# Sliding-window attention and a sentence-level MoE: an FFN schedule with its short slots moved back, and another order of the load queue

## The chip, the cores and the metric

One core of a Trainium2 chip runs the whole program: a matmul engine (TensorE, PE), three engines for elementwise work and reductions (VectorE or DVE, ScalarE or ACT, GpSimd or POOL), SyncE, and 16 DMA engines that all transfers share. The metric is the device time of one launch in microseconds, here the median of three runs.

## The reference, cut to what matters

Eight sentences (batches) of 576 tokens. First comes attention with 8 heads of width 64. Heads 0 to 3 look back over a window of 32 tokens ("plain"), heads 4 to 7 over 128 tokens at every fourth one ("dual", for dilated). The result, 576 x 512 per batch, is averaged over its tokens; a gate picks one of eight experts for the whole batch; and this expert's two-layer FFN with ReLU runs on all tokens of the batch.

```python
def _attn_ref(q, k, v):                     # each (8, 8, 576, 64) f32
    scores = scale * np.matmul(q, k.transpose(0, 1, 3, 2))
    rel = pos[:, None] - pos[None, :]
    mask_plain = (rel >= 0) & (rel < 32)
    mask_dil = (rel >= 0) & (rel < 128) & (rel % 4 == 0)
    ...                                     # softmax over the masked scores
    return np.matmul(attn, v)

def _moe_ref(x, w_gate, w1, w2):            # x (8, 576, 512), w1 (8, 512, 1024), w2 (8, 1024, 512)
    pooled = x.mean(axis=1)
    logits = pooled @ w_gate
    e_idx = np.argmax(logits, axis=1)       # one expert for a whole batch
    ...
    h = np.maximum(x[mask] @ w1[e], 0.0)
    out[mask] = gate_w[mask, None, None] * (h @ w2[e])
```

So no weight of batch b can be loaded before the attention of batch b is over, its mean is taken and the gate has named an expert.

## The kernel before: slots, pieces, gate and queue

Each batch's attention is cut into four slots of two heads (slot t has batch t // 4; the first two of a batch are dual, the last two plain), and its FFN into 21 pieces: 16 of the first layer (8 column blocks x 2 halves of the tokens, four matmuls each), four of the second (128 tokens each, eight matmuls) and a tail of 64 tokens. `PIECES` says how many pieces run beside each attention slot. PE works in this order strictly.

```python
PIECES = [0] * 7 + [6, 6, 5, 2, 2] + [8, 8, 2, 3] * 7
```

FFN 0 so runs in slots 7 to 11, and FFN b in slots 4b+8 to 4b+11. Attention ends in slot 31 (the last output of it in slot 32), and slots 32 to 39 have FFN 6 and FFN 7 alone.

One slot of the main loop, cut; `pre` is the slot before, whose second half ends here:

```python
for t in range(7, len(PIECES)):
    cur, pre = sl[t], sl[t - 1]
    ...                                    # items = the pieces of this slot
    gb, gn = divmod(t - 5, NSLOT)
    if gn == 0 and 0 < gb < B:
        emit_gate(gb)                      # gate of batch b at the start of slot 4b+5
    ...
        run_T(t)                           # transposes of keys or queries for a slot to come (L267)
        pre.av_a()                         # probabilities x values, first part (L353)
        flush()                            # stores of finished output tiles
        cur.s()                            # scores (L288)
        cur.x()                            # exp (ACT)
        pre.av_b()
        if lead: items.pop(0)()
        pre.ln(); cur.mask(); pre.rd()
    for f in items[:k0]: f()
    pre.norm()                             # normalise, and sum for the mean (DVE)
    for b, g, nm in tsched.get(t + 1, []):
        if g == 0:
            emit_pair(b, nm)               # rearrange plain keys or queries on DVE (L251)
    for f in items[k0:]: f()
```

`tsched` places the transposes: dual keys of batch b in slot 4b-2, dual queries in 4b-1, plain keys in 4b, plain queries in 4b+1. For the plain ones `emit_pair` reads the loaded tile one slot earlier, on DVE.

The gate, with the loads that hang on it. All loads of the program are issued by GpSimd, one after the other, and turn f32 into bf16 on the way:

```python
def emit_gate(b):
    ...                                    # 4 matmuls, maximum and index (DVE), the index to a GpSimd register
    nc.gpsimd.dma_start(out=w1b[:, 2:4, :], ...)            # w1 of the chosen expert, L511
    for a in range(2):
        nc.gpsimd.dma_start(out=w1b[half(a), 0:2, :], ...)  # its other half in two parts, L516
    if b == 0:
        load_va(2)                         # dual values of batch 2
        load_qb(2)                         # plain keys and queries of batch 2
        load_w2(e_val, w2b)
        load_qa(3)                         # dual keys and queries of batch 3
        load_vb(2)                         # plain values of batch 2
    else:
        load_vb(b + 2)                     # plain values
        load_w2(e_val, w2b)
        load_qa(b + 3)                     # dual keys, dual queries
    load_va(b + 3)                         # dual values
    load_qb(b + 3)                         # plain keys, plain queries
```

GpSimd waits in this queue for the expert's index before it goes on to w1 of batch b and to everything listed after it.

The first layer, where w1's four row blocks are taken in the order in which they land:

```python
def ffn1(b, fc, hf, eng, cs=(2, 3, 0, 1)):
    ...
    if 2 in cs:
        s["hm"] = bank()[:, 0:HALF]        # one of three PSUM banks
    hm = s["hm"]
    for c in cs:
        ...
        nc.tensor.matmul(hm, lhsT=w[:, fc % 4, :], rhs=s["xt"][:, c, cols], start=(c == 2), stop=(c == 1))   # L573
    if 1 not in cs:
        return
    ...                                    # ReLU to bf16, on ACT or DVE
```

Of the kernel before, what the change touches and what calls it, by code (L numbers as in the profile page):

```python
# [20 lines left out]
B = 8  # L21
# [21 lines left out]
HALF = 288  # L43
NSLOT = 4
EARLY = 7

PIECES = [0] * 7 + [6, 6, 5, 2, 2] + [8, 8, 2, 3] * 7


@with_exitstack  # L50
def kernel(
# [42 lines left out]
    def bank():  # L94
        return psM.tile([P, 512], F32, name="m", tag="M", space=PSUM)[:]
# [12 lines left out]
    def load_tiles(b):  # L108
        t = {}
        for g in range(2):  # L110
            for nm in ("k", "q"):
                shape = [P, RJ, DH] if g else [P, 2, RH, DH]
                t[nm, g] = ldp.tile(shape, BF16, name=f"{nm}m{g}", tag=f"{nm}m{g}")
            t["v", g] = ldp.tile([P, 4, 4, DH], BF16, name=f"vm{g}", tag=f"vm{g}")
        t["vt", 0] = ldp.tile([KB, 4, DH], BF16, name="vt0", tag="vt0")
        t["vt", 1] = ldp.tile([KB, 4, 2, DH], BF16, name="vt1", tag="vt1")
        loads[b] = t

    def load_1(b, g, nm):
        i = src[nm][b, 4 * g : 4 * g + 4]  # L120
        if g == 0:
            i = bass.AP(tensor=i.tensor, offset=i.offset, ap=[[RH * DH, P], [2 * S * DH, 2], [1, RH * DH]])
            nc.gpsimd.dma_start(out=loads[b][nm, g][:].rearrange("p h j d -> p h (j d)"), in_=i)
        else:
            i = i.rearrange("h s d -> (h s) d").rearrange("(p j) d -> p j d", j=RJ)
            nc.gpsimd.dma_start(out=loads[b][nm, g][:], in_=i)

    def load_qk(b, g):
        for nm in ("k", "q"):
            load_1(b, g, nm)  # L130

    def load_v(b, g):
        t = loads[b]["v", g]
        if g == 0:
            for h in range(4):
                nc.gpsimd.dma_start(out=t[:, h], in_=v[b, h, 0:512, :].rearrange("(c p) d -> p c d", p=P))  # L136
        else:
            nc.gpsimd.dma_start(out=t[:], in_=v[b, 4:8, 0:512, :].rearrange("h (p j) d -> p h j d", j=4))

    def load_vt(b, g):  # L140

        vt = loads[b]["vt", g]
        if g == 0:
            nc.gpsimd.dma_start(out=vt[:], in_=v[b, 0:4, 512:S, :].rearrange("h p d -> p h d"))
        else:
            nc.gpsimd.dma_start(out=vt[:], in_=v[b, 4:8, 448:S, :].rearrange("h (p t) d -> p h t d", t=2))

    GO = (1, 0)

    def load_qa(b):  # L150
        if b < B:
            load_tiles(b)
            load_qk(b, GO[0])

    def load_va(b):
        if b < B:
            load_v(b, GO[0])
            load_vt(b, GO[0])

    def load_qb(b):  # L160
        if b < B:
            load_qk(b, GO[1])

    def load_vb(b):
        if b < B:
            load_v(b, GO[1])
            load_vt(b, GO[1])
# [75 lines left out]
    def half(a):  # L243
        return slice(64 * a, 64 * a + 64)
# [250 lines left out]
    def emit_gate(b):  # L495
        s = st[b]
        pooled = s["pooled"]
        lg = bank()[0:1, 0:E]
        for c in range(4):
            nc.tensor.matmul(lg, lhsT=pooled[:, c : c + 1], rhs=wg_t[:, c, :], start=(c == 0), stop=(c == 3))  # L500
        l_sb = small.tile([1, E], F32, name="l_sb", tag="l_sb")
        mx = small.tile([1, 8], F32, name="mx", tag="mx")
        mi = small.tile([1, 8], U32, name="mi", tag="mi")
        nc.vector.max_with_indices(mx[:], mi[:], lg)
        nc.vector.tensor_copy(out=l_sb[:], in_=lg)
        s["gate"] = (l_sb, mx)
        e_val = nc.values_load(mi[0:1, 0:1].bitcast(I32), engines=[ET.Pool], min_val=0, max_val=E - 1)
        w2b = wp.tile([P, 8, DM], BF16, name="w2b", tag="w2b")
        w1b = wp.tile([P, 4, F], BF16, name="w1b", tag="w1b")
        s["w1"], s["w2"] = w1b, w2b  # L510
        nc.gpsimd.dma_start(  # L511
            out=w1b[:, 2:4, :],
            in_=moe_w1[ds(e_val, 1), 256:512, :].rearrange("e (c p) f -> p (e c) f", p=P),
        )
        for a in range(2):
            nc.gpsimd.dma_start(  # L516
                out=w1b[half(a), 0:2, :],
                in_=moe_w1[ds(e_val, 1), 128 * a : 128 * a + 128, :].rearrange("e (h d) f -> d (e h) f", d=DH),
            )
        if b == 0:  # L520
            load_va(2)
            load_qb(2)
            load_w2(e_val, w2b)
            load_qa(3)
            load_vb(2)
        else:
            load_vb(b + 2)
            load_w2(e_val, w2b)
            load_qa(b + 3)
        load_va(b + 3)  # L530
        load_qb(b + 3)

    def load_w2(e_val, w2b):

        nc.gpsimd.dma_start(
            out=w2b[:].rearrange("p (x j) f -> p x (j f)", x=2),
            in_=moe_w2[ds(e_val, 1)].rearrange("e (x p j) f -> p (e x) (j f)", x=2, p=P),
        )
# [16 lines left out]
    def emit_gate_bc(b):  # L555

        gw = st[b]["gw"]
        gbc = small.tile([P, 1], F32, name="gbc", tag="gbc")
        nc.sync.dma_start(out=gbc[:], in_=gw[0:1, 0:1].to_broadcast([1, P]))
        st[b]["gbc"] = gbc  # L560


    def ffn1(b, fc, hf, eng, cs=(2, 3, 0, 1)):
        s = st[b]
        if fc == 0 and hf == 0 and "ht" not in s:
            s["ht"] = htp.tile([P, 8, S], BF16, name="ht", tag="ht")
        cols = slice(HALF * hf, HALF * hf + HALF)
        if 2 in cs:
            s["hm"] = bank()[:, 0:HALF]
        hm = s["hm"]  # L570
        for c in cs:
            w = s["w1"][:, c, F // 2 * (fc // 4) : F // 2 * (fc // 4) + F // 2].rearrange("p (m j) -> p j m", j=4)
            nc.tensor.matmul(hm, lhsT=w[:, fc % 4, :], rhs=s["xt"][:, c, cols], start=(c == 2), stop=(c == 1))  # L573
        if 1 not in cs:
            return
        o = s["ht"][:, fc, cols]
        if eng == "A":
            nc.scalar.activation(out=o, in_=hm, func=AF.Relu)  # L578
        else:
            nc.vector.tensor_scalar_max(out=o, in0=hm, scalar1=0.0)  # L580
# [3 lines left out]
    def flush():  # L584
        for f in stores:
            f()
        stores.clear()
# [40 lines left out]
    for b in range(B):  # L628
        for n in (0, 2):
            t = NSLOT * b + n  # L630
# [3 lines left out]
    def run_T(t):  # L634
        for b, g, nm in tsched.get(t, []):
            for f in emit_T(b, g, nm):
                f()
# [41 lines left out]

    sl = [slot(t) for t in range(len(PIECES))]  # L680

# [10 lines left out]
    nd_banks = {"0dk": (0, 1), "0pk": (0, 1), "1dk": (2, 1), "1dq": (0, 2)}  # L692
    evac = {}

    def piece(b, x, e):
        if x < 16:
            ffn1(b, x // 2, x % 2, e)
        elif x < 20:
            ffn2(b, x - 16, "AD"[x % 2])
        else:  # L700
            ffn_tail(b)
# [35 lines left out]
    done = 0  # L737
    for t in range(7, len(PIECES)):
        cur, pre = sl[t], sl[t - 1]
        n = PIECES[t]  # L740

        lead = t > 7 and n >= 5 and done % 21 < 16 and pre.on
        items = []
        for i, x in enumerate(range(done, done + n)):
            e = "A" if ((lead or t == 7) and i == 0) or 2 * i >= n else "D"
            items.append(lambda x=x, e=e: piece(x // 21, x % 21, e))
        done += n
        gb, gn = divmod(t - 5, NSLOT)
        if gn == 0 and 0 < gb < B:
            emit_gate(gb)  # L750
        if t == 7:
            items.pop(0)
            n -= 1
            dve, act = emit_T(2, GO[0], "q")
            dve()
            act()
        else:
            run_T(t)
            pre.av_a()
            flush()  # L760
            if (t == 8) if gb == 0 else gn == 2 and gb < B:
                emit_gate_bc(gb)
            cur.s()
            cur.x()
            if pre.on and not cur.on:
                items.pop(0)()
                n -= 1
            pre.av_b()
            if lead:
                items.pop(0)()  # L770
                n -= 1
            pre.ln()
            cur.mask()
            pre.rd()
        k0 = n // 2
        for f in items[:k0]:
            f()
        if t > 7:
            pre.norm()
        for b, g, nm in tsched.get(t + 1, []):  # L780
            if g == 0:
                emit_pair(b, nm)
        for f in items[k0:]:
            f()
        if (t == 7) if gb == 0 else gn == 1 and gb < B:
            emit_gate_w(gb)
# [31 lines left out]
```

The softmax here doesn't subtract the row's maximum and nothing guards it: scores larger than these inputs give would overflow.

## Time and profile before

| what | value |
|---|---|
| median of 3 runs | 212.21 us (212.17 to 212.45) |
| span of the profiled execution | 210.9 us |
| PE busy | 192.6 us, 91% |
| load queue's packets (q0) | 31.2 MB written, 96.2% of 16 engines' span |
| first layer, L573 | 512 matmuls, 67.2 us |
| second layer, L593 | 56.9 us |

The page cuts the span into 40 slices of 5.27 us and gives the busy share of each engine in tenths. "DMA" there is the mean busy share of the 16 engines; "PEclk" is the clock that PE was granted. The chain of waits goes back from the last instruction, at each step to what released it; a DMA in it is counted from its issue to its landing. A wait is written "engine line <- what released it: total us, times, longest".

### The profile page before, as it was taken

To read this page: it belongs to the slowest core of one execution; us is meant where nothing else is said; L and a number is where in the kernel's file an instruction comes from. 1 tells how busy PE (TensorE), PEld (TensorE's weight loads), DVE (VectorE), ACT (ScalarE), POOL (GpSimd) and SP (SyncE) were. 2 spreads that over 40 slices of the span, in tenths; PEclk is the share of its full clock that TensorE was granted. 3 is DMA by queue.
4 is the path that set the end of the run, shared out by engine and by line. 5 is a ranking of instruction groups with operands and counts; after the bars stand their busy time and mean duration, and the time that the engine had idled before them with its cause. 6 is when DMAs were issued, how large, how long until landed. Compare 5 with 4: busy or idle time off the path is not lost.

```text
span 210.9 us, 6979 instructions
## 1 busy us (share of the span) xinstructions
PE 192.6 (91%) x2906; PEld 140.1 (66%) x2921; DVE 129.6 (61%) x359; ACT 135.0 (64%) x270; POOL 82.4 (39%) x130
## 2 busy tenths in 40 slices
PE   6866979989969999999999998989999999999991
PEld 1645757975658755895598656876589558749741
DVE  5476868676767657766777466765777465325312
ACT  2497796976648766886678864876698656332320
POOL 7977385239236262626362253626104000500000
PEclk9996557999999999999999999999999999999998
DMA  5999999999999999999999999999999994499223
GB/s 70 184 182 197 171 172 199 216 185 168 209 228 235 207 210 230 221 243 208 221 215 246 208 211 222 236 228 209 235 204 203 215 217 139 75 215 231 106 113 111
DMA packets 46415, 41.11 MB, mean 195 GB/s; under 512 B 24880, under 2 KB 34096, under 8 KB 46384
## 3 DMA queue, kind: packets, MB, share of 16 engines
q0 software_dynamic: 38784, 31.20, 96.2%
q1 hardware_dynamic: 7600, 9.46, 13.9%
q8 instruction: 23, 0.38, 0.7%
q14 instruction: 8, 0.07, 0.1%
HBM read 62.41 MB, written 9.44 MB: 341 GB/s over the span
## 4 chain that ended last, share of the span: by engine, by line
PE 58%; DMA 30%; issue 4%; ACT 2%; DVE 2%; POOL 1%; POOLq 1%; SPq 0%
PE m L573 21%; PE m L593 20%; DMA w1b<-in_moe_w_dram 15%; DMA qm<-in_q_dram 9%; DMA km<-in_k_dram 6%; PE n L353 5%; PE m L267 4%; PE m L608 3%; PE ps L288 2%; PE n L267 1%; PE m L500 1%; ACT pt L321 1%; ACT rd L468 1%; PE m L353 1%; DVE pt L328 1%
## 5 line engine op out<-in xcount | busy, mean ns | idle before, releaser
L573 PE MATMUL m<-xt,w1b 128*128 128x288 bf16 x512 | 67.2, 288 | 2.1 <-DMA w1b<-in_moe_w_dram 1.6
L573 PEld LDWEIGHTS <-w1b 128*128 128x128 bf16 x512 | 56.5, 114 | 8.1 <-issue 3.2
L593 PE MATMUL m<-w2b,ht 128*128 128x512 bf16 x241 | 56.9, 379 | 0.9 <-issue 0.2
L578 ACT ACTIVATE ht<-m 128x288 bf16<-128x288 f32 x77 | 31.6, 411 | 21.3 <-PE m L573 17.6
L593 PEld LDWEIGHTS <-ht 128*128 128x128 bf16 x256 | 24.1, 98 | 27.3
L484 DVE SCALAR_TENSOR_TENSOR xt<-n,rd 128x512 bf16<-128x512 f32 (+3 forms) x58 | 29.4, 545 | 10.1 <-ACT rd L468 10.1
L328 DVE TENSOR_TENSOR pt<-pt,mk 128x896 bf16<-128x896 bf16 x32 | 20.0, 625 | 21.7 <-ACT pt L321 21.7
L275 ACT ACTIVATE qk<-m 128x512 bf16<-128x512 bf16 (+1 forms) x27 | 19.9, 739 | 16.9 <-PE m L267 16.8
L321 ACT ACTIVATE pt<-ps 128x896 bf16<-128x896 f32 x32 | 29.0, 905 | 2.8 <-PE ps L288 2.8
L136 POOL DMA_DIRECT2D vm<-in_v_dram x32 | 24.0, 763 | 10.8 <-DMA qm<-in_q_dram 4.3
L272 DVE COPY qk<-m 128x640 bf16<-128x640 bf16 (+1 forms) x29 | 23.0, 797 | 6.7 <-PE m L267 6.6
L580 DVE TENSOR_SCALAR ht<-m 128x288 bf16<-128x288 f32 x51 | 22.8, 456 | 6.4 <-PE m L573 5.4
L600 DVE TENSOR_SCALAR osb<-m,gbc 128x512 f32<-128x512 f32 x16 | 12.0, 750 | 17.6 <-PE m L593 17.6
L468 ACT ACTIVATE rd<-lnd 128x576 f32<-128x576 f32 x32 | 21.9, 684 | 1.0
L353 PE MATMUL n<-pt,ones 64*64 64x64 bf16 (+6 forms) x262 | 21.2, 250 | 1.2 <-DVE pt L328 1.0
L463 ACT ACTIVATE lnd<-n 128x512 f32<-128x512 f32 (+3 forms) x58 | 20.6, 406 | 0.9 <-PE n L353 0.9
L511 POOL DMA_DIRECT2D w1b<-in_moe_w_dram x8 | 5.7, 716 | 38.3 <-DVE ht L580 18.0
L353 PE MATMUL n<-pt,vm 64*64 64x96 bf16 (+3 forms) x606 | 20.4, 203 | 0.2
L353 PEld LDWEIGHTS <-vm 64*64 64x64 bf16 x672 | 15.7, 112 | 3.3 <-SPq L421 1.5
L598 ACT ACTIVATE osb<-m,gbc 128x512 f32<-128x512 f32 x16 | 10.9, 682 | 8.7 <-PE m L593 8.7
L353 PEld LDWEIGHTS <-ones 64*64 64x64 bf16 x288 | 12.7, 112 | 5.3 <-issue 1.9
L288 PE MATMUL ps<-qk 64*64 64x96 bf16 (+3 forms) x608 | 14.9, 210 | 1.3 <-ACT pt L321 1.1
(72 smaller groups left out, 199.7 us busy)
## 6 DMA issues: line engine op xcount, KB each, us to landing
w2b<-in_moe_w_dram POOLq DMA_DIRECT2D x8, 1024.0 KB, 11.5
out_dram<-osb SPq DMA_DIRECT2D x32, 256.0 KB, 6.9
km<-in_k_dram POOLq DMA_DIRECT2D x16, 288.0 KB, 11.6
qm<-in_q_dram POOLq DMA_DIRECT2D x16, 288.0 KB, 11.5
w1b<-in_moe_w_dram POOLq DMA_DIRECT2D x8, 512.0 KB, 11.5
w1b<-in_moe_w_dram POOLq DMA_DIRECT2D x16, 256.0 KB, 11.0
vm<-in_v_dram POOLq DMA_DIRECT2D x8, 256.0 KB, 9.6
vm<-in_v_dram POOLq DMA_DIRECT2D x32, 64.0 KB, 10.1
```

The source lines that it names most:

```text
L136: nc.gpsimd.dma_start(out=t[:, h], in_=v[b, h, 0:512, :].rearrange("(c p) d -> p c d", p=P))
L272: nc.vector.tensor_copy(out=ev[x][0], in_=ev[x][1])
L321: nc.scalar.activation(out=pt[:], in_=s["ps"][:, :, 0:NP], func=AF.Exp, scale=0.125)
L328: nc.vector.tensor_tensor(out=pt[:], in0=pt[:], in1=mk[:, g : g + 1, :].to_broadcast([P, 2, NP]), op=ALU.mult)
L353: x = nc.tensor.matmul(oo, lhsT=lhsT, rhs=rhs, start=start, stop=True, skip_group_check=True)
L463: nc.scalar.activation(out=lnd[:, lo : lo + w], in_=ndc(o, w), func=AF.Ln)
L468: nc.scalar.activation(out=rd[:], in_=s["lnd", n][:], func=AF.Exp, scale=-1.0)
L484: nc.vector.scalar_tensor_tensor(out=o, in0=i0, scalar=1.0, in1=i1, op0=ALU.mult, op1=ALU.mult, accum_out=s["pool"][:, w, c : c + 1])
L573: nc.tensor.matmul(hm, lhsT=w[:, fc % 4, :], rhs=s["xt"][:, c, cols], start=(c == 2), stop=(c == 1))
L578: nc.scalar.activation(out=o, in_=hm, func=AF.Relu)
L580: nc.vector.tensor_scalar_max(out=o, in0=hm, scalar1=0.0)
L593: nc.tensor.matmul(om, lhsT=s["ht"][:, fc, r * P : (r + 1) * P], rhs=s["w2"][:, fc, :], start=(fc == 0), stop=(fc == 7))
```

## The change

The slot list is shifted: FFN 0 to FFN 4 run with 8, 8, 2 and 3 pieces a slot from slot 7 on, so that FFN b starts in slot 4b+7, seven slots after its attention began, not eight. The slots with few pieces, formerly 7 to 11, are now 27 to 31, where FFN 5 is spread over five slots. FFN 6 and FFN 7 stay in slots 32 to 39. With the attention nearer to its FFN, the plain keys and queries are loaded one gate later, and the queue behind a gate is put in the order in which its loads are needed: w1, plain keys, w2, plain queries, dual keys, plain values, dual queries, dual values. The gate is now emitted ahead of the last piece of slot 4b+4. The first two pieces of an FFN are interleaved, so that both use the half of w1 that lands first before either needs the rest.

```diff
-PIECES = [0] * 7 + [6, 6, 5, 2, 2] + [8, 8, 2, 3] * 7
+PIECES = [0] * 7 + [8, 8, 2, 3] * 5 + [6, 6, 4, 3, 2] + [8, 8, 2, 3] * 2
 ...
+        near, far = b + 2 < B, b + 3 < B
+        if near:
+            load_1(b + 2, GO[1], "k")
+        load_w2(e_val, w2b)
         if b == 0:
             load_va(2)
-            load_qb(2)
-            load_w2(e_val, w2b)
-            load_qa(3)
-            load_vb(2)
-        else:
+        if near:
+            load_1(b + 2, GO[1], "q")
+        if far:
+            load_tiles(b + 3)
+            load_1(b + 3, GO[0], "k")
+        if near:
             load_vb(b + 2)
-            load_w2(e_val, w2b)
-            load_qa(b + 3)
-        load_va(b + 3)
-        load_qb(b + 3)
+        if far:
+            load_1(b + 3, GO[0], "q")
+            load_va(b + 3)
 ...
         if 2 in cs:
-            s["hm"] = bank()[:, 0:HALF]
-        hm = s["hm"]
+            s["hm", fc, hf] = bank()[:, 0:HALF]
+        hm = s["hm", fc, hf]
 ...
-            items.append(lambda x=x, e=e: piece(x // 21, x % 21, e))
+            if x % 21 == 0 and t > 7:
+                items.append(lambda x=x, e=e: (piece(x // 21, 0, e, (2, 3)), piece(x // 21, 1, e, (2, 3)), piece(x // 21, 0, e, (0, 1))))
+            elif x % 21 == 1 and t > 7:
+                items.append(lambda x=x, e=e: piece(x // 21, 1, e, (0, 1)))
+            else:
+                items.append(lambda x=x, e=e: piece(x // 21, x % 21, e))
 ...
-        if gn == 0 and 0 < gb < B:
-            emit_gate(gb)
 ...
-        for f in items[k0:]:
+        for i, f in enumerate(items[k0:]):
+            if i == len(items) - k0 - 1 and t % NSLOT == 0 and t // NSLOT - 1 < B:
+                emit_gate(t // NSLOT - 1)
             f()
```

## The prediction

> **What bounds the kernel now.** I read the page first, then the chain of waits in order of time, then TensorE's (PE's) waits, then single transfers. From the page:
>
> ```profile
> PE 192.6 (91%) x2906; PEld 140.1 (66%) x2921; DVE 129.6 (61%) x359; ACT 135.0 (64%) x270; POOL 82.4 (39%) x130
> ...
> PEclk9996557999999999999999999999999999999998
> DMA  5999999999999999999999999999999994499223
> ...
> q0 software_dynamic: 38784, 31.20, 96.2%
> ```
>
> Two things are full at once: PE is busy 91% of the span, and the DMA row stands at 9 from slice 2 to slice 33 (about 5 to 174 us). The half clock of slices 4 to 7 lies ahead of the first FFN; the change starts after it. The chain shows where one or the other leads (start us, us, what):
>
> ```profile
> 49.74 12.06 DMA w1b<-in_moe_w_dram
> ...
> 84.67 4.04 PE m L573 x32
> ...
> 107.00 4.04 PE m L573 x32
> ...
> 128.87 12.27 DMA km<-in_k_dram
> 141.14 0.05 issue
> 141.19 0.68 PE m L267 x9
> ...
> 158.08 0.61 PE m L267 x9
> ...
> 206.60 0.48 DVE osx L617
> ```
>
> The chain comes back to the load queue at 61.80 (w1 of batch 1) and 141.14 (dual keys of batch 7); from 141.19 to 206.60 it is PE alone. An FFN starts every 107.00 - 84.67 = 22.33 us when PE leads. The load queue needs a little more: the third w1 transfer of batch 1 lands at 49.74 + 12.06 = 61.80, that of batch 5 at 152.7 (issued at 141.43, 11.3 us to landing in its own view), so 90.9 / 4 = 22.7 us per batch. Hence PE's waits after 38 us are few and short:
>
> ```profile
> PE m L573 <- DMA w1b<-in_moe_w_dram: 1.6, 2, 1.0
> PE m L267 <- DMA km<-in_k_dram: 1.0, 2, 0.8
> PE m L267 <- DVE kx L251: 1.0, 1, 1.0
> PE m L500 <- ACT ht L578: 0.5, 1, 0.5
> PE m L267 <- ACT ht L578: 0.4, 1, 0.4
> PE m L593 <- issue: 0.2, 1, 0.2
> ```
>
> They add up to 4.7 us. That is all the change can win after 38 us, for it neither adds nor removes a matmul. The load rate comes from the stages without stores, 120 to 126 and 142 to 149 us (the last two columns are DMA share and GB/s):
>
> ```profile
> 120.00:126.00 6.00, 5.95 (x78) 3.37 (x78) 3.69 (x11) 4.09 (x9) 3.61 (x5) 1.00 1.17 213
> 142.00:149.00 7.00, 6.89 (x132) 4.15 (x121) 4.16 (x11) 5.09 (x11) 3.63 (x6) 1.00 1.19 208
> ```
>
> Some 210 GB/s of bf16 are written; twice that is read, since the loads turn f32 into bf16. Last, two rows of GpSimd's (POOL's) timeline: the issue of w1 for batch 4, and of w2 for batch 5:
>
> ```profile
> 113.12 0.72 POOL L511 DMA_DIRECT2D w1b<-in_moe_w_dram  x1 [2.38 <-PE n L353]
> ...
> 150.52 0.70 POOL L535 DMA_DIRECT2D w2b<-in_moe_w_dram  x1 [2.54 <-DMA w1b<-in_moe_w_dram]
> ```
>
> The gate's matmuls of batch 4 began at 111.05 in the chain, so a gate is worth a w1 issue 2.1 us later. In its own view the w2 of 150.52 takes 11.2 us and lands at 161.7.
>
> **What the Trainium skill says.** "DMA: Bandwidth & Descriptors", section "Bandwidth", gives 425 GB/s for one core's large loads, issued from GpSimd. Here the read side is 2 x 210 = 420 GB/s: it agrees, and no order of the queue will raise the rate. The same page, "Issuing engines are not separate DMA queues", says that transfers of all issuers share the 16 DMA engines; the trace agrees, for w2 of batch 0, with hardly a store beside it, lands 5.4 us behind the load ahead of it, the one of batch 5, with stores, 6.1 us behind. "TensorE: Matmul & The Clock Gate", section "Architectural detail: the array is 16× 32×32, not 1× 128×128", calls VectorE (DVE) and ScalarE strict FIFO. The trace before has every wait in program order, but shows no DVE held by a late load, so this it does not test; I use it below for the pair copy.
>
> **The change part by part.**
>
> (1) PIECES. The FFN of batches 1 to 5 starts one slot earlier; of 6 and 7 in the same slot as before, because slots 27 to 31 spread FFN 5 over five slots. After slot 31 both have the same 42 pieces left. So at FFN 1 PE has one attention slot less behind it: the parts around 158.08 are 0.61 + 0.39 + 0.23 + 0.34 = 1.57 us. That slot is only moved; it is done later.
>
> (2) The queue. Ahead of w1 of batch b stood everything of batches up to b+1, the dual part of b+2, and the plain keys and queries of b+2. Those two now follow w1. Each is 288 KB (page), 0.295 MB at 210 GB/s = 1.4 us, so in a full queue w1 lands 2.8 us earlier: FFN 1 near 61.8 - 2.8 = 59.0. PE comes there some 2.6 us earlier than its 60.5, the first w1 matmul before (1.6 for the slot, 1.0 for the wait for kx, which arose behind a short slot of 2 pieces). FFN 1 is thus worth about 2.5 us at its start, less the 1.57 still owed.
>
> (3) The price is the plain queries. Before, those of batch 7 landed at 147.1 (issued 133.74, 13.3 us in their own view), 11 us ahead of their transpose at 158.08. Now they stand behind w1, the plain keys and w2 of batch 5. Everything issued by then is what had been issued up to w2 of batch 5 before, less the plain values of batch 7 (4 x 64 + 32 KB, 1.4 us). So in a queue that never ran dry they land at 161.7 - 1.4 = 160.3. A copy on DVE rearranges the pair (0.46 us in the DVE rows before), so the transpose of slot 29 starts near 160.8.
>
> (4) When would PE be there? Before, 158.08. It now carries 12 pieces of FFN 5 ahead of slot 29 instead of 8: four pieces of 4.04 / 8 = 0.505 us, 2.0 in all. Without any of the 4.7 us of waits: 158.1 + 2.0 - 4.7 = 155.4. The load at 160.8 ends last: PE stands still for up to 5 us, in this slot or in shares at the plain queries of earlier batches.
>
> (5) The rest. From 158.08 to the end of the last matmul, 206.58, were 48.5 us without a gap that counts. Four pieces are already done: 46.5. Last matmul 160.8 + 46.5 = 207.3. The tail to the span's end is 210.9 - 206.6 = 4.3, and the measured time is 212.2 - 210.9 = 1.3 over the span: 207.3 + 5.6 = 212.9.
>
> (6) The split of the first two pieces lets four matmuls (0.5 us) run on w1's first transfer instead of two; it takes a second PSUM bank for half a microsecond. Worth at most 0.25 us where w1 is late; it doesn't add up behind (4). The gate moves from the start of slot 4b+5 to ahead of the last piece of slot 4b+4: half a microsecond or so.
>
> **The rivals.**
>
> A. The load queue leads at the plain queries, as above: 212.9. For it: 22.7 against 22.33 us per batch, and the DMA row. Against it: near 53 us the w1 of batch 1 came slowly (8.7 us for all three transfers after the plain queries of batch 3 had landed, 5.6 for those of batch 2), and if that does not recur, 1 to 2 us come back: 211.
>
> B. PE leads throughout: all of the 4.7 us go, and slot 29 starts at 155.4. 155.4 + 46.5 + 5.6 = 207.5. Against it: it needs the queue 5 us faster, at a rate that is already at its ceiling. Small.
>
> C. The gate becomes the bound. From gate to its FFN, PE had 84.67 - 65.77 = 18.9 us; now one piece (0.5), the second half of an FFN (8.1: at 165 to 174, 3.56 twice and 0.99) and three slots' attention (4.2) are left, 12.8 us. The issue takes 2.1, and a w1 behind a queue as full as before lands 11 us after that, its third part 3 us later still: too late by 3 us. But POOL's wait at the gate lets the queue run down to some 5 us, so w1 comes as the stream brings it, no later. Only if the queue runs empty at each gate is time lost for good: 1 us at four gates makes 217. A DVE that waits for the plain queries also holds the gate's maximum behind it, which works the same way.
>
> **Range and chances.** A is by far the likeliest, between 211 and 214 with its own uncertainty (the 161.7 carries stores, the slow stretch may go or stay). B or something near it, 10%; C, 12%. I take 212.7, and 209.5 to 216.0 as the range. Faster by over 2% needs less than 208.0, nearly all of B: 0.05. Slower by over 2% needs more than 216.5, all of C: 0.08. Same: 0.87.
>
> **What would show it.** In the new profile: FFN 1 starting at 58 to 60; FFN 5's start 2 to 4 us earlier than 153.76; POOL waiting longer at the gates; PE's waits for w1 and dual keys gone and in their place waits of the transposes (L267) for qx or the plain queries, the longest in slot 29, with its start at 159 to 162; from there 46.5 us to the last matmul. I am wrong if slot 29 starts at 156 without a wait (then B), or if the DMA row shows holes behind the gates and FFN 2 to 5 come more than 23 us apart (then C).

## The result, and the profile after

| | median | lowest to highest |
|---|---|---|
| before, beside it | 212.19 us | 211.51 to 212.45, 4 runs |
| after | 219.88 us | 219.05 to 220.62, 4 runs |

The ratio is 1.037, with a 95% interval of 1.032 to 1.041: the change costs 7.7 us, where 0.5 had been predicted. The profiled span is 218.0 us, against 210.9.

The page of the kernel after, the same rows as of before:

```profile
PE 196.4 (90%) x2921; PEld 140.9 (65%) x2921; DVE 129.5 (59%) x359; ACT 135.5 (62%) x270; POOL 82.5 (38%) x130
...
PEclk9955557999999999999999999999996999999998
DMA  5999999999999999999999999999996993399223
...
q0 software_dynamic: 38784, 31.20, 94.0%
```

The load queue has no hole at any gate up to slice 30 (163 us), just as before. PEclk has a new 6 in slice 31, a stretch of half clock late in the program that the kernel before doesn't have.

The chain of waits, from 73 us on and at the end (start us, us, what):

```profile
73.96 0.71 POOL qm L123
74.67 18.09 DMA km<-in_k_dram
97.15 0.71 POOL w2b L541
97.86 17.64 DMA qm<-in_q_dram
...
121.75 17.48 DMA qm<-in_q_dram
...
145.78 17.80 DMA qm<-in_q_dram
164.12 0.78 PE m L267 x9
...
212.65 1.01 PE m L614 x16
```

Where the chain of before came back to the queue twice after 38 us and was PE alone from 141 us on, it now runs from load to load. The four long ones land at 92.76, 115.50, 139.23 and 163.58; three of them are the plain queries, and the last is followed at 164.12 by the transpose of slot 29. PE's waits of the kernel after between 38 and 172 us say the same (total us, times, longest):

```profile
PE m L267 <- DVE qx L251: 4.6, 4, 1.6
PE m L500 <- DVE pooled L492: 0.9, 1, 0.9
PE m L267 <- DVE kx L251: 0.8, 1, 0.8
PE n L353 <- ACT ht L584: 0.5, 1, 0.5
```

The waits for w1 are gone, as meant. The four for rearranged plain queries (0.86 us at 91.89, 1.27 at 116.05, 0.85 at 139.77, 1.63 at 164.12) have taken their place, and below them stand three that are not of the queue's making. The starts of the FFNs, read as the first matmul of each in the traces, give a ledger of the whole loss; all figures are us from one start to the next (starts rounded to 0.1 us), and the last column goes from FFN 6 to the end of the last matmul:

| kernel | 0 to 1 | 1 to 2 | 2 to 3 | 3 to 4 | 4 to 5 | 5 to 6 | 6 to end |
|---|---|---|---|---|---|---|---|
| before | 28.3 | 24.1 | 22.3 | 22.7 | 24.1 | 20.2 | 32.7 |
| after | 25.6 | 22.6 | 23.8 | 24.2 | 23.7 | 28.3 | 32.8 |

Two things stand in it. Up to FFN 5 the sum of the differences is -1.6 us, which is no more than the one attention slot (1.57 us) that is still owed: of the 4.2 us won up to FFN 2, 3.0 are given back by FFN 4. And between FFN 5 and FFN 6, where the short slots now are, 8.1 us are lost, five times the slot. The experiments ask for the cause of each.

### The profile page after: what moved, and what is told of

Same layout as the page of the kernel before. It is cut to its first block, busy times and chain, and to the rows that moved or that the text cites. A ratio compares the mean times of both kernels' runs of the same rounds, so it can differ in the third digit from the quotient of the medians.

```text
span 218.0 us, 6994 instructions
## 1 busy us (share of the span) xinstructions
PE 196.4 (90%) x2921; PEld 140.9 (65%) x2921; DVE 129.5 (59%) x359; ACT 135.5 (62%) x270; POOL 82.5 (38%) x130
## 4 chain that ended last, share of the span: by engine, by line
PE 40%; DMA 38%; issue 6%; POOL 5%; DVE 5%; ACT 3%; POOLq 1%; SPq 0%
DMA qm<-in_q_dram 27%; PE m L579 16%; PE m L599 13%; DMA km<-in_k_dram 8%; PE n L353 4%; DMA w1b<-in_moe_w_dram 3%; PE m L267 3%; POOL w1b L516 2%; DVE qk L272 1%; PE m L614 1%; POOL w2b L541 1%; PE ps L288 1%; DVE qx L251 1%; ACT qk L275 1%; DVE xt L484 1%
## 5 line engine op out<-in xcount | busy, mean ns | idle before, releaser
L579 PE MATMUL m<-xt,w1b 128*128 128x288 bf16 x512 | 69.6, 292 | 0.6 <-ACT qk L275 0.3
L599 PE MATMUL m<-w2b,ht 128*128 128x512 bf16 x256 | 57.7, 380 | 0.0
L584 ACT ACTIVATE ht<-m 128x288 bf16<-128x288 f32 x77 | 31.3, 410 | 24.2 <-PE m L579 21.0
L136 POOL DMA_DIRECT2D vm<-in_v_dram x32 | 24.2, 768 | 22.3 <-DMA w1b<-in_moe_w_dram 12.6
L272 DVE COPY qk<-m 128x640 bf16<-128x640 bf16 (+1 forms) x29 | 23.2, 802 | 5.7 <-PE m L267 5.3
L586 DVE TENSOR_SCALAR ht<-m 128x288 bf16<-128x288 f32 x51 | 21.7, 453 | 6.0 <-PE m L579 5.6
L353 PE MATMUL n<-pt,ones 64*64 64x64 bf16 (+6 forms) x262 | 22.3, 259 | 1.0 <-DVE pt L328 0.8
L353 PE MATMUL n<-pt,vm 64*64 64x96 bf16 (+3 forms) x606 | 21.0, 207 | 1.0 <-ACT ht L584 0.5
L353 PEld LDWEIGHTS <-vm 64*64 64x64 bf16 x672 | 16.6, 117 | 4.6 <-SPq L421 1.8
L288 PE MATMUL ps<-qk 64*64 64x96 bf16 (+3 forms) x608 | 15.5, 213 | 1.4 <-ACT pt L321 0.8
L353 PEld LDWEIGHTS <-ones 64*64 64x64 bf16 x288 | 13.3, 117 | 4.8 <-issue 1.5
```

What stands on the lines that cost most here:

```text
L272: nc.vector.tensor_copy(out=ev[x][0], in_=ev[x][1])
L353: x = nc.tensor.matmul(oo, lhsT=lhsT, rhs=rhs, start=start, stop=True, skip_group_check=True)
L599: nc.tensor.matmul(om, lhsT=s["ht"][:, fc, r * P : (r + 1) * P], rhs=s["w2"][:, fc, :], start=(fc == 0), stop=(fc == 7))
```

## The experiments

Every ratio is to the kernel before, run beside it on the same chip, with its 95% interval. Periods of w1 are taken from the landings of its third transfer, batch 2 to batch 5, divided by three.

### Each half of the change by itself

The first run keeps the new schedule and puts the old queue order back; the second keeps the old schedule and takes the new order.

```diff
 # sched_old_queue: the kernel after with
-        near, far = b + 2 < B, b + 3 < B
-        ...                            # w1, plain keys, w2, plain queries, dual keys, ...
+        if b == 0: ...                 # the whole order of before
 # queue_alone: the kernel before with the new order in that place
```

> The changed kernel (219.9 us) with the queue order of before: plain keys and queries one gate earlier, ahead of w1. Theory Q (the plain queries behind w2 hold up the transposes, the schedule is innocent): the waits for qx go, the stream returns to some 22.7 us per batch, 211 to 214 us. Rival S (the shorter way from a gate to its FFN costs the time, whatever the order): w1 then lands 2.8 us later than in the changed kernel and PE waits for it at each FFN, 218 us or more.

> The kernel before (212.2 us) with the new queue order alone. Theory Q: the plain queries, now behind w1, plain keys and w2, are needed one slot after the FFN starts, but the gate lies a slot further ahead of it: waits for qx of a microsecond or so a batch, 214 to 218 us. Rival S: without the shorter way nothing is lost, 211 to 213 us.

Measured: sched_old_queue 217.28 us, ratio 1.029 (1.024 to 1.034); queue_alone 213.95 us, ratio 1.011 (1.007 to 1.016).

| kernel | 0 to 1 | 1 to 2 | 2 to 3 | 3 to 4 | 4 to 5 | 5 to 6 | 6 to end |
|---|---|---|---|---|---|---|---|
| sched_old_queue | 25.7 | 25.2 | 22.6 | 22.6 | 23.3 | 25.7 | 32.8 |
| queue_alone | 28.8 | 23.6 | 22.4 | 23.3 | 22.8 | 21.0 | 32.7 |

PE's waits of sched_old_queue, 38 to 172 us:

```profile
PE m L575 <- DMA w1b<-in_moe_w_dram: 3.0, 2, 2.5
PE n L353 <- DVE xt L484: 1.0, 1, 1.0
PE m L500 <- DVE pooled L492: 0.9, 1, 0.9
PE m L267 <- DVE kx L251: 0.8, 1, 0.8
```

What follows. Neither theory came true whole: the stream returned, as Q had it, but the time stayed near S. The schedule alone costs most of the loss, 5.8 of the 7.7 us. (It is the slot list with the gate's new place and the split pieces; the split was not run by itself.) With the old queue, w1's period is 23.0 us as in the kernel before, the wait for it at FFN 1 is the 2.5 of the first line, and the stretch from FFN 5 to FFN 6 still takes 25.7 us. A whole slot more would make it 20.2 + 1.57 = 21.8; 3.9 us are lost beyond that, and 3.0 of them are the last three lines and one more wait of 0.31 for xt at 177.26. None of these four waits is for a load: they are for the pair copy, the sum for the mean, and the normalised tile. The queue alone costs some 2.4 us (1.5 to 3.3) and holds 23.1 us a batch. So in these two traces neither half makes the 24 us of the kernel after.

### Does it help to move the plain queries?

```diff
 # q_before_w2: the kernel after; before_q_first: the kernel before with the new order; in both
+        if near:
+            load_1(b + 2, GO[1], "q")
         load_w2(e_val, w2b)
         if b == 0:
             load_va(2)
-        if near:
-            load_1(b + 2, GO[1], "q")
```

> The changed kernel with the plain queries ahead of w2 in the queue, not behind it. Theory Q: they land some 6 us earlier (w2 takes 5.8), the waits for qx (0.9, 1.3, 0.8 and 1.6 us) go, w2 comes 2 us later and is just in time: 211 to 214 us. If the load stream itself is slower (23.9 us per batch against 22.7), whatever order is inside a group, the waits move to w2 or to w1 and the time stays over 217 us.

> The kernel before with the new queue, but plain queries ahead of w2 (slots, gate and pieces as before). With the new queue alone PE waited 4.7 us for copies of plain keys and queries, 3.7 of that for queries behind w2; w1 landed 5 us before its FFN. Theory Q: those 3.7 us go and nothing takes their place: 208.5 to 210.5 us, under the kernel before. Rival (the load stream's own rate sets the time): 212 to 214 us.

Measured: q_before_w2 218.43 us, ratio 1.033 (1.024 to 1.042), with runs from 216.23, the profiled one, to 221.85; before_q_first 211.73 us, ratio 0.999 (0.997 to 1.002). In the first, the waits for plain queries are gone, and PE waits for something else of the same queue (38 to 172 us):

```profile
PE m L579 <- DMA w1b<-in_moe_w_dram: 2.5, 3, 1.0
PE n L353 <- DVE xt L484: 1.0, 1, 1.0
PE m L500 <- DVE pooled L492: 0.9, 1, 0.9
PE m L267 <- DVE kx L251: 0.9, 1, 0.9
```

What follows. w1 still comes every 23.9 us, even in the fastest run. A stream that is late is late for whatever is next in need; taking one wait away moves most of it: PE waits 5.3 us here between 38 and 172 us, 6.8 in the kernel after. On the old schedule the same order costs no time. But in its trace w1 comes every 23.6 us and PE waits 3.6 us for plain keys, so a slower stream doesn't need the new schedule.

### The short slots

In the kernel after, the slots with few pieces are 27 to 31. Four runs move or drop them:

```diff
-PIECES = [0] * 7 + [8, 8, 2, 3] * 5 + [6, 6, 4, 3, 2] + [8, 8, 2, 3] * 2
+PIECES = [0] * 7 + [8, 8, 2, 3] * 5 + [8, 8, 2, 3, 0] + [8, 8, 2, 3] * 2   # no_thin_late
+PIECES = [0] * 7 + [8, 8, 2, 3] * 8                                       # no_thin, no_thin_q
+PIECES = [0] * 7 + [8, 8, 2, 3] * 2 + [6, 6, 4, 3, 2] + [8, 8, 2, 3] * 5   # thin_mid_q
```

The names that end in q also have the plain queries ahead of w2.

> The changed kernel with slots 27 to 31 at 8, 8, 2, 3 and 0 pieces instead of 6, 6, 4, 3, 2. Theory T (a slot with few pieces late in the program leaves PE to wait for the chain of exp, mask, sum and normalisation on ACT and DVE): the waits for kx (0.8 us), the gate (0.9) and ACT or DVE in slot 30 (0.5 to 1.0) go, and the plain queries of batch 7 are needed 2 us later: 215.5 to 218 us. Rival: the stream of loads alone sets slot 29, then only its neighbours change: 219 to 221 us.

> The changed kernel without any thin slots: 8, 8, 2 and 3 pieces from slot 7 to the end, one slot fewer in all; FFN 6 then starts in slot 31 and FFN 7 in slot 35. Theory T (spreading FFN 5 over five slots leaves PE to wait for the chain of exp, mask, sum and normalisation on ACT and DVE, some 3 us in slots 28 to 32, whatever the queue): those waits go, the wait for the last plain queries stays: 215.5 to 218 us. Rival (the attention that is left has to be run in any case and its chain only moves): 219 to 221 us.

> No thin slots, and the plain queries ahead of w2. Both costs together: theory T with theory Q gives 213 to 216 us, with waits for w1 at each FFN left (0.7 to 1.0 us each, as with the plain queries ahead of w2 alone). Rival (the load stream at 24 us per batch sets the end): 217 us or more.

> The plain queries ahead of w2, and the five thin slots at FFN 2 (slots 15 to 19) instead of FFN 5; FFN 3 to 7 then start in slot 4b+8 as in the kernel before. Theory T: thin slots cost some 3 us wherever PE has no gap to fill, but from FFN 3 on w1 has a slot more and its waits (2.5 us) go: 213.5 to 216 us. Rival (only the end of the program is sensitive to them): 211 to 213 us.

Measured: no_thin_late 222.07 us, ratio 1.046 (1.041 to 1.051); no_thin 221.44, ratio 1.044 (1.040 to 1.048); no_thin_q 217.65, ratio 1.028 (1.025 to 1.031); thin_mid_q 214.63, ratio 1.018 (1.013 to 1.023). The profiles of no_thin_late and no_thin_q are of disturbed executions and are not compared. PE's waits of no_thin, 38 to 205 us:

```profile
PE m L267 <- DVE qx L251: 4.1, 3, 1.7
PE m L579 <- DMA w1b<-in_moe_w_dram: 2.5, 1, 2.5
```

The waits for the gate, for kx and for xt of the short slots are gone. FFN 7, now at seven slots' distance too, waits 2.5 us for w1 instead, and PE runs at half clock from 117.5 to 120.9 and, after that wait, from 199.5 to 202.9. Its FFN 5 to FFN 6 takes 23.6 us, FFN 6 to the end of the last matmul 37.7. Of thin_mid_q the starts of the FFNs:

| kernel | 0 to 1 | 1 to 2 | 2 to 3 | 3 to 4 | 4 to 5 | 5 to 6 | 6 to end |
|---|---|---|---|---|---|---|---|
| thin_mid_q | 26.2 | 22.6 | 27.6 | 23.0 | 22.7 | 20.6 | 32.8 |

What follows. The idea that without the short slots the late loss simply disappears fell in no_thin and no_thin_q, which have none: what no_thin saves, late loads and half clock take. At both places tried PE loses more than the slot's own 1.57 us; in thin_mid_q FFN 2 takes 27.6 us, 3.7 more than the 22.3 of the kernel before and the slot. In the kernel before they stand at slots 7 to 11, ahead of FFN 1, and PE's waits of 0.54 and 0.98 us there come before w1 lands at 61.80, for which PE waits another 0.98. And from slot 20 on, where thin_mid_q is at eight slots' distance again, the periods are 23.0 and below and no wait for w1 or plain queries is left, with the new queue order and the plain queries ahead of w2. So the long period isn't tied to the place in the program; the seven slots together with the new order go with it, but that they are its cause isn't shown.

### Is it the gate?

Rival C of the prediction. In the kernel after DVE takes the pair copy of the plain queries ahead of the gate's maximum. DVE's timeline of the kernel after at the gate of batch 4 (its matmuls run at 113.81):

```profile
113.50 0.16 DVE L492 TENSOR_TENSOR pooled<-pool 128x4 f32<-128x4 f32 x1
115.53 0.46 DVE L251 COPY qx<-qm 128x1152 bf16<-128x1152 bf16 x1 [1.86 <-DMA qm<-in_q_dram]
115.90 0.15 DVE L504 MAX8 mx<-m 1x8 f32<-1x8 f32 x1
```

DVE stands 1.86 us for a load with the maximum ready behind it. And GpSimd's at the same gate:

```profile
113.53 0.55 POOL L126 DMA_DIRECT2D qm<-in_q_dram  x1 [5.37 <-DMA w2b<-in_moe_w_dram]
115.79 0.74 POOL L138 DMA_DIRECT2D vm<-in_v_dram  x1 [1.72 <-DMA qm<-in_q_dram]
117.19 0.62 POOL L146 DMA_DIRECT2D vt<-in_v_dram  x1 [0.66 <-DMA km<-in_k_dram]
118.45 0.70 POOL L511 DMA_DIRECT2D w1b<-in_moe_w_dram  x1 [0.64 <-PE n L353]
```

w1 goes out at 118.45, 4.6 us after the gate's matmuls. The brackets show what each issue waited for last. The first three are landings, of w2, the plain queries and the dual keys, each the load eight before the one to be issued. Over the whole trace no more than eight loads are outstanding at any time, and eight is also the largest number in the kernel before. So GpSimd comes to w1 late even when the gate's answer is there. Four runs take the gate apart:

```diff
 # gate_ahead_of_pair: the kernel after, in slots with a gate
-        emit_pair(...)                      # ahead of the pieces and the gate
+        emit_pair(...)                      # behind them
 # gate_old_place: the kernel after
+        if gn == 0 and 0 < gb < B:
+            emit_gate(gb)                   # at the start of slot 4b+5, as before
 ...
-            if i == len(items) - k0 - 1 and t % NSLOT == 0 and t // NSLOT - 1 < B:
-                emit_gate(t // NSLOT - 1)
 # after_fixed_expert, before_fixed_expert:
-        e_val = nc.values_load(mi[0:1, 0:1].bitcast(I32), engines=[ET.Pool], ...)
+        e_val = b
```

> The changed kernel with the copy of the plain queries behind the gate on DVE, so that the gate's maximum doesn't wait for their landing (1.9 us at batch 3). Rival C of the prediction (the gate held on DVE delays w1 and with it the stream): 1 to 2 us per batch come back, 213 to 216 us. Theory Q: GpSimd stands at the dual values' issue until the dual keys land anyway, so w1 is issued no earlier: 219 to 220 us.

> The changed kernel with the gate back at the start of slot 4b+5. The wait of PE for the mean in slot 28 (0.9 us) goes, and w1 is asked for half a microsecond later. Theory T: 218.5 to 219.5 us, hardly a change, since the copy of the plain queries holds DVE at the gate anyway. Rival C (the gate's place sets the loop of gate, w1 and FFN): 221 us or more.

> The kernel after, with the expert's number fixed to the batch's own number, so that the loads of w1 and w2 need not wait for the gate (the choice of expert is left out, so the output isn't the reference's). Theory L (at seven slots' distance the loads go round a loop: FFN, then gate, then w1, then the next FFN, with so short a stretch of loads queued that the order of issues is held to the gate): the third part of w1 comes back to 22.5 to 23.0 us a batch, the waits for plain queries of 0.86 to 1.63 us go, and the time falls to 212 to 216 us. Theory P (the packets themselves go slower in this order, whatever the gate does): w1 stays at 23.7 to 24.1 us a batch and the time at 218 to 221 us.

> The kernel before with the expert's number fixed in the same way, as a control. Theory L: its loop has slack, so the w1 landings stay near 22.7 us a batch and the time is 210 to 212.5 us. Theory P: the same. If it gains over 3 us, the gate costs both kernels and the gain of the run on the kernel after must be cut by as much.

Measured: gate_ahead_of_pair 220.75 us, ratio 1.043 (1.035 to 1.050); gate_old_place 221.58, ratio 1.047 (1.043 to 1.051); before_fixed_expert 210.50, ratio 0.993 (0.991 to 0.995). The two with a fixed expert leave out the gate's choice. after_fixed_expert has no ratio: three of its four runs, the profiled one among them, took 220.78 to 223.96 us and one 213.46.

What follows. Freeing DVE gains nothing. A later gate costs 1.7 us more than the kernel after, with waits for plain queries of 7.7 us in place of 4.6, so the gate isn't without weight. The fixed expert decides nothing: 213.46 is what theory L forecast, the three others are at or over what P forecast, and the only trace is of the slowest, 223.96. There the stream takes 25.0 us a batch though nothing waits for a gate, so it can be slow without one. Whether the gate's wait makes it slow in the kernel after, and what the execution of 213.46 did otherwise, is open.

### Size and number of the plain values' transfers

The plain values come as four transfers of 64 KB in packets of 128 bytes. In the "wide" kernels a partition takes four neighbouring rows, so packets have 512 bytes; the rows then stand in another order and the output isn't the reference's, but bytes and matmuls are the same.

```diff
-            for h in range(4):
-                nc.gpsimd.dma_start(out=t[:, h], in_=v[b, h, 0:512, :].rearrange("(c p) d -> p c d", p=P))
+            # after_wide_v, before_wide_v: one transfer
+            nc.gpsimd.dma_start(out=t[:], in_=v[b, 0:4, 0:512, :].rearrange("h (p j) d -> p h j d", j=4))
+            # after_wide_v4, before_wide_v4: the same packets in four transfers
+            for h in range(4):
+                nc.gpsimd.dma_start(out=t[:, h], in_=v[b, h, 0:512, :].rearrange("(p c) d -> p c d", c=4))
 # after_w1_one: the kernel after
-        nc.gpsimd.dma_start(out=w1b[:, 2:4, :], ...)
-        for a in range(2):
-            nc.gpsimd.dma_start(out=w1b[half(a), 0:2, :], ...)
+        nc.gpsimd.dma_start(out=w1b[:], in_=moe_w1[ds(e_val, 1)].rearrange("e (c p) f -> p (e c) f", p=P))
```

> The changed kernel with the plain values of a batch loaded in one transfer of 512-byte packets instead of four of 128-byte packets; the value rows then stand in another order, so the plain heads' output is not the reference's; all shapes and matmuls are the same. Theory R (the stream fell from 22.7 to 23.9 us per batch for want of rate: 128-byte packets by themselves move 145 to 160 GB/s, and w1's packets slow down beside their issue): the batch falls to 22.7 or less and the time by 4 us or more, 212 to 216 us. Rival (a loop of gate, w1 and queries sets 23.9): 218 to 220 us.

> The kernel before with the same wide load of plain values (rows in another order, so the plain heads' output is not the reference's). Theory R: its stream, too, has less to do, but PE leads there: 208 to 211 us, a gain clearly smaller than the changed kernel's. Rival: the same gain in both.

> The kernel after with the plain values in packets of 512 bytes, but still in four transfers a batch (rows in another order in the tile, so the output isn't the reference's); the earlier run with wide packets had also merged the four transfers into one. If the packet size is what the 4.2 us of that run came from: 215 to 217 us, and w1 at 23.0 to 23.3 us a batch. If it was the smaller number of transfers, of which only eight are outstanding at a time: 218.5 to 220.5 us, w1 at 23.8 to 24.1.

> The kernel before with the plain values in packets of 512 bytes in four transfers (rows in another order in the tile, so the output isn't the reference's); with the same packets in one transfer it took 209.4 us. Theory N, if the limit of eight binds the kernel before too: 211.5 to 213 us, no gain. If before has slack at the limit and the gain came from the packets: 209 to 210 us.

> The kernel after with w1 in one transfer of 1 MB in place of three (two of the four row blocks come in another order, so the output isn't the reference's); the bytes, the packets of 2 KB and every other load stay. Theory N (at most eight loads are outstanding, and in this order the ones behind w1 are small, so that the number of transfers a batch sets how early the next ones are issued): with 11 loads a batch in place of 13 the w1 landings come to 23.0 to 23.4 us a batch and the time to 215 to 217.5 us. Against it (the order of bytes or the FFN's own loop sets the 24 us): landings stay at 23.8 to 24.2 a batch and the time at 218.5 to 221 us.

| kernel | median us | ratio | w1's period, us | one 2-KB packet of w1, ns |
|---|---|---|---|---|
| before | 212.19 | | 23.0 | 173 |
| sched_old_queue | 217.28 | 1.029 | 23.0 | 173 |
| queue_alone | 213.95 | 1.011 | 23.1 | 175 |
| before_wide_v4 | 210.28 | 0.992 (0.989 to 0.996) | 22.8 | 173 |
| thin_mid_q | 214.63 | 1.018 | 23.2 | 178 |
| before_q_first | 211.73 | 0.999 | 23.6 | 183 |
| after_wide_v | 215.73 | 1.020 (1.016 to 1.024) | 23.1 | 184 |
| q_before_w2 | 218.43 | 1.033 | 23.9 | 194 |
| after_w1_one | 221.70 | 1.044 (1.039 to 1.050) | 23.7 | 200 |
| after | 219.88 | 1.037 | 24.1 | 200 |
| after_wide_v4 | 222.80 | 1.049 (1.045 to 1.053) | 24.4 | 207 |
| after_fixed_expert | 221.43 | none | 25.0 | 214 |

before_wide_v took 209.40 us, ratio 0.988 (0.984 to 0.991). The last column is the mean of the trace's DMA records over the same three batches. Both explanations that went into these runs fell. Wide packets by themselves gain nothing on the kernel after (222.80), though they gain on the kernel before, in four transfers (210.28) as in one. And two transfers fewer gain nothing either (after_w1_one, whose first piece has to wait for all of w1, 1.0 us in all; it takes w1's rows in another order, so its output isn't the reference's either). Only one wide transfer helps, by 4.2 us. On the kernel before it gains 2.1 us (211.54 to 209.40), so about half of that isn't particular to the kernel after.

The two kernels with one wide transfer show the change on a faster stream. From 38 us on PE waits for no load in either; after_wide_v has left, from 38 to 172 us:

```profile
PE n L352 <- DVE xt L483: 1.0, 1, 1.0
PE m L499 <- DVE pooled L491: 0.9, 1, 0.9
PE m L266 <- DVE kx L250: 0.8, 1, 0.8
PE m L266 <- ACT ht L583: 0.5, 1, 0.5
```

Yet after_wide_v takes 6.3 us more than before_wide_v. From the start of FFN 5 to the end of the last matmul are 58.7 us (149.03 to 207.77) against 52.9 (150.36 to 203.23); sched_old_queue has 58.5 there. So most of the loss is the schedule's, in its last stretch, and the slow stream comes on top.

The last two columns say where the stream is slow. The period goes roughly with the mean duration of w1's own packets. A batch has 512 of them on 16 engines, so 200 ns for 173 makes 512 x 27 / 16 = 0.86 us, of the 1.05 us by which the period grew. The packets of w2 (4 KB) took 323 ns in the kernel after and 335 before, those of the plain values 32 in both. So the queue isn't idle, and it isn't slow everywhere: it is slow while w1 comes. The stretches of both kernels in which w1 comes alone show it. The kernel after:

```profile
98.00:100.00 2.00, 2.00 (x45) 1.19 (x36) 1.33 (x2) 1.97 (x5) 1.92 (x3) 1.00 1.11 203
100.00:102.00 2.00, 2.00 (x11) 0.78 (x8) 1.21 (x4) 1.21 (x2) 0.74 (x1) 1.00 1.11 163
76.00:78.00 2.00, 2.00 (x11) 0.90 (x10) 1.31 (x5) 1.42 (x3) 0.76 (x2) 1.00 1.09 160
```

The kernel before:

```profile
98.00:100.00 2.00, 2.00 (x17) 1.13 (x15) 1.54 (x5) 0.63 (x1) 1.66 (x3) 1.00 1.19 217
77.00:79.00 2.00, 1.98 (x60) 1.52 (x60) 1.17 (x5) 0.83 (x3) 1.25 (x2) 1.00 1.14 214
```

With nearly the same DMA share (the column before the last), 160 GB/s pass in place of 203 to 217. In both slow lines PE has 11 matmuls in 2 us: it is in the second layer of the FFN before, whose matmuls have 512 columns. Take the half microseconds from 40 us on in which at least 20 packets of w1 start and at most two of other loads or stores. In the kernel after, w1's packets average over 200 ns in 19 of 49 of them with a second layer on PE, and in none of 7 with attention alone. But the kernel before has 35 with a second layer, and only 3 are slow. And thin_mid_q has both kinds with the same work on PE:

```profile
76.00:78.00 2.00, 2.00 (x11) 0.88 (x9) 1.31 (x5) 1.37 (x3) 0.60 (x1) 1.00 1.06 165
98.00:100.00 2.00, 2.00 (x11) 0.94 (x10) 1.22 (x4) 1.10 (x2) 1.75 (x3) 1.00 1.11 207
```

So meeting the second layer goes with it and isn't enough for it. What makes these packets slow is open.

### A version that beats both

The kernel before waits 1.0 us for dual keys, which stand behind w2, although w2 is needed later:

```diff
 # before_kd_first: the kernel before
             load_vb(b + 2)
+            load_tiles(b + 3)
+            load_1(b + 3, GO[0], "k")
             load_w2(e_val, w2b)
-            load_qa(b + 3)
+            load_1(b + 3, GO[0], "q")
```

> The kernel before with the dual keys of the batch after next issued ahead of w2 and the rest of its queue order kept. If the order of w2 and the dual keys costs it its waits of about 1 us for dual keys: 210.3 to 211.6 us. If the wait only moves to w2 or to the queries: 211.7 to 213 us.

Measured: 211.38 us, ratio 0.996 (0.995 to 0.998). PE's waits, 38 to 172 us:

```profile
PE m L577 <- DMA w1b<-in_moe_w_dram: 2.6, 2, 1.5
PE m L267 <- DVE kx L251: 1.0, 1, 1.0
```

The wait for dual keys is gone; the one for w1 grew from 1.6 to 2.6. The gain, 0.4%, is small but measured, and it is the lowest ratio with the full computation here. The 209.40 us of before_wide_v show what one wide transfer could bring, if keys and masks were put in its row order too; that was not tried.

## Why the prediction was wrong, point by point

**Step (1), the moved slot: right at the front, wrong at the back.** FFN 1 starts at 58.2. "That slot is only moved; it is done later" holds up to FFN 5, where the debt is 1.6 us; FFN 5, expected 2 to 4 us earlier than 153.76, started at 152.49, 1.3 earlier. What the step took for granted is that the five short slots cost the same at 27 to 31 as at 7 to 11. They don't: with the old queue 3.9 us beyond the slot, 3.0 of them in four waits for work of DVE and ACT.

**Step (2), the queue up to w1: right in direction, too small.** The third part of w1 of batch 1 landed at 56.7, 5.1 us earlier where 2.8 were worked out. The slow stretch near 53 us that rival A named didn't come back in that length.

**Step (3), the plain queries: the mechanism was right, the size was not.** They do end last. The term that failed is "in a queue that never ran dry they land at 161.7 - 1.4 = 160.3". The queue didn't run dry, and they landed at 163.58. From the first w1 of the loop to the last, (152.6 - 56.7) / 4 = 24.0 us a batch took the place of 22.7: 4 x 1.3 = 5.2 us lost, against 59.0 - 56.7 = 2.3 won in step (2), leaves 2.9 of the 3.3. I had taken the rate of the stream as a constant that "no order of the queue will raise", and forgot that a schedule may lower it. The stretches that gave 213 and 208 GB/s before, 120 to 126 and 142 to 149 us, now read:

```profile
120.00:126.00 6.00, 6.00 (x86) 3.33 (x83) 4.29 (x11) 3.80 (x7) 3.81 (x6) 1.00 1.12 177
142.00:149.00 7.00, 7.00 (x90) 3.83 (x88) 4.46 (x9) 5.40 (x11) 5.79 (x9) 1.00 1.21 184
```

The Trainium skill, "DMA: Bandwidth & Descriptors", section "Bandwidth", gives rates by the size of a transfer and not by what the engines do meanwhile. Here the same transfers of w1 were written at 203 to 217 GB/s in some stretches and at 160 in others, so its 425 GB/s was a ceiling, as I used it, and no floor.

**Step (4), PE without waits at 155.4: too early.** In after_wide_v, where from 38 us on PE waits for no load, the transpose of slot 29 starts at 159.06, with 2.2 us of waits for ACT and DVE ahead of it (0.46, 0.81 and 0.93), of which the step has none. In the kernel after PE was there at 162.49 and the queries still ended last, as said; the standing still of up to 5 us came as the 4.6 us of the four waits.

**Step (5), "the rest": 46.5 us from the transpose of slot 29 to the last matmul. It took 49.5** (164.12 to 213.66), 3.0 more. The kernel after around that point (columns as before; the third number from the right is the clock):

```profile
162.00:165.20 3.20, 1.57 (x43) 1.10 (x45) 1.41 (x6) 0.67 (x2) 0.00 (x0) 1.00 1.58 108
165.20:168.60 3.40, 3.40 (x51) 2.37 (x43) 1.69 (x5) 2.69 (x5) 2.62 (x4) 0.50 0.37 51
168.60:172.00 3.40, 2.92 (x67) 1.90 (x65) 1.59 (x6) 2.21 (x5) 0.00 (x0) 1.00 1.11 205
```

PE waited 0.94 us for the gate's mean at 161.53 and 1.63 for the plain queries; then it ran 3.4 us at half clock, which by itself costs up to 1.7 us. But the same stretch takes 48.7 us in sched_old_queue (161.75 to 210.45) and in after_wide_v (159.06 to 207.77), where the clock stays full and the last plain queries aren't waited for. So the term that failed is the 46.5 itself, carried over from slots with another share of pieces: 2.2 of the 3.0 us come with the new schedule, 1.2 to 1.3 of them as waits for xt (0.98 and 0.31 in sched_old_queue, 0.98 and 0.21 in after_wide_v), the remaining 0.9 unexplained. The half clock adds 0.8 net, beside shorter waits (0.48 and 0.31).

The Trainium skill, "TensorE: Matmul & The Clock Gate", section "Part 1: The HAM clock gate (the "warmup" mystery)", puts the return to half clock at an idle window of some 3.4 us. The length agrees; but PE was busy 1.57 of the 3.2 us before it, so here about half a window of waits was enough. Elsewhere it wasn't: in sched_old_queue PE waits 2.5 us for w1 at FFN 1 and keeps its full clock:

```profile
58.20:61.60 3.40, 0.92 (x9) 0.63 (x8) 1.27 (x2) 0.93 (x2) 0.91 (x2) 1.00 1.76 214
61.60:65.00 3.40, 3.40 (x31) 3.00 (x30) 2.59 (x8) 2.97 (x8) 2.62 (x4) 1.00 1.15 276
```

A wait can so have a second price, and the prediction counted only the first; when it falls due these runs don't show.

**Step (6), split pieces and gate: no sign either way.** The waits for w1 that the split was to shorten don't occur, and the earlier gate, put at half a microsecond, gains about what gate_old_place loses, 1.7 us.

**The rivals.** A had the right bound and too fast a stream. B had no part. C had the right symptom, FFN 2 to 5 are 23.8, 24.2 and 23.7 us apart, and even the 217 of its size; its mechanism, holes behind the gates, isn't there. DVE was held by the plain queries ahead of the gate's maximum, as C said, and as the strict FIFO of the section cited in the prediction has it (1.86 us in the trace after); it didn't set the time, for gate_ahead_of_pair gained nothing.

**The sum.** Transpose of slot 29 3.3 us later than predicted, the rest 3.0 longer, tail and time outside the span 6.2 for 5.6 (219.88 - 213.66), and 0.2 between the 212.9 of the working and the 212.7 on record: 7.1 of the 7.2 us between 219.88 and 212.7. What is known of causes: most of the loss is the schedule's, 5.8 us with the old queue (sched_old_queue) and 6.3 with one wide transfer in both kernels. Some 4 us of it are lost where the short slots now stand, beyond their own work. The slower stream, with its wait at slot 29 and the half clock that followed, brings the remaining 1.4 to 1.9. The shares overlap: while the stream is slow, dropping the short slots gains nothing (no_thin). Why w1's packets are slow at seven slots' distance with the new order is not settled.

## What to carry to other kernels

Slots with little work are slack, and slack is worth what it hides: where the short slots stood before, PE had w1 of FFN 1 to wait for in any case, and moved to where PE is full they cost some 4 us beyond their own work. A stream that is "full" can still be slower than it was: compare GB/s over the stretch of one tile's transfer before taking the old rate over to a new schedule. And before two kinds of change go in together, run each alone: here neither half shows what the two together do to the stream.

## What the runs showed of the hardware

- Packets of 2 KB of w1 take 173 ns on average in the kernel before. In the kernel after, in stretches of one to three microseconds, their half-microsecond means rise to 200 to 245 ns, with all 16 engines at work and hardly another transfer beside them (160 GB/s in place of 203 to 217). At 148 to 150 us there most still take 173 ns, and a third take 205 to 653.
- Less than a whole window's wait can bring the half clock, and need not: 3.4 us of it came after 3.2 us in which PE was busy for 1.57 (after), none after 3.4 us in which it was busy for 0.92 (sched_old_queue).
- GpSimd never has more than eight loads outstanding in these programs. The issue of a load waits for the landing of the one eight before it, so w1's issue stood behind those of smaller loads (118.45 us, 4.6 us after its gate). That this cost time isn't shown, as the queue ran on meanwhile.
